# Moving the last zero fill behind the value gradient and w_q stores and giving six transfer engines more of it

## The chip, the cores and the metric

The kernel runs on one core of one Trainium2 chip. A core has five engines that take instructions (PE for matrix products, DVE and ACT for element-wise work, POOL, and SP), and sixteen transfer engines that carry out the DMAs which POOL, SP and ACT request. The metric is the device time of one execution in microseconds (us). The kernel before takes 594.82 us, the median of three runs (594.19 to 594.88).

## The reference

The reference is one decode step of a small transformer block, forward and backward, with batch and sequence of 1 and width D = 1024. Forward: six modulation vectors come from `silu(c) @ w_mod`; a layer norm scaled and shifted by two of them feeds attention of 32 query heads over 4 groups of cached keys and values, of which only the last 4096 of 65536 rows are used; the result goes through `wo`, a gate vector and a residual sum; a second layer norm feeds a gated feed-forward part (`sigmoid(h w_gate) * (h w_up)` times `w_down`) with its own gate and residual sum. Backward: given `grad_out`, it returns the output and the gradients by x, both caches, wq, wo, w_gate, w_up, w_down, c and w_mod.

Two things in this set the amount of data moved. The gradient of a weight matrix is, with one row of activations, an outer product of two vectors, and it has to be written in full. And the gradients of the two caches have the shape of the whole cache, (1, 4, 65536, 128) in bf16, 64 MB each, although only the last 4096 rows of each group are not zero. The other 61440 rows of each of 8 groups (15 MB a group, 120 MB in all) must be written as zeros. The kernel writes 186 MB in all and reads 79 MB.

## The kernel before, in words

**Zero fills.** The 120 MB of zeros are cut into pieces of 1 MB (`zleft`, filled at lines 149 to 156) and each is written by one DMA, or a few, that POOL requests. The helper `zero(n)` at line 185 takes n pieces from the list and issues them at the place in the program where it is called; tables such as `Z_N`, `Z_B`, `Z_FFN` and `Z_ROWS` (lines 51 to 59) say how many go at each place, so that the fills run beside loads and computation over the whole kernel. A fill has one of these forms: the plain one (line 209) writes 128 rows of 8 KB, cast from a tile of zeros in SBUF, eight rows to each of the sixteen transfer engines; the big one (line 203) copies 32 rows of 32 KB from a region of DRAM that was filled earlier (`zero_src`); six "narrow" ones (lines 191 to 199) use only 120 rows, shared out over fifteen engines, so that one engine is passed over. A fourth form, `uneven` (line 171), is in the file, and is used for the pieces whose running number stands in `UNEVEN`; that tuple is empty.

**How a piece is given to certain engines.** A DMA whose outermost count is not a multiple of sixteen is spread over fewer engines, beginning where the previous such DMA left off. Before an uneven or narrow fill POOL executes an instruction that puts this place back to the start (`reset_dge_cursor`, lines 174 and 192). `uneven` then issues very small DMAs only to move the place on (7 and 6 partitions), and larger ones that go to few engines.

**Order.** The whole kernel is written under a manual schedule: each engine executes its instructions in the order of the source, and waits are placed where data depend on each other. All transfers that POOL requests go through one software queue (q0), those of SP through a hardware queue (q1); both are served by the same sixteen transfer engines.

**The last quarter of the kernel**, in the order of POOL's requests: stores of outer products for w_down (`dwd`, line 1132), w_up and w_gate (`dw_rows`, line 1127), wo (`dwo`, line 1262) with fills between them (`Z_ROWS[0]` at line 1226, `Z_ROWS[1]` at line 1332); then the sections of w_mod (`sec`, line 1256) and the tiles of w_q (`dwq_tile`, line 1306); the value gradient (`grad_kv` at line 1431, stored by `kv_store`, line 1303, group 3 at line 1441); then the eighth section and the fourth w_q tile, `dwq_tile(3)` (line 1443); and last the key gradient (line 1481) with the other four w_q tiles and the first two w_mod columns (`s2`, line 1310) between its steps. From the third quarter of the key gradient on the stores are requested by SP (`tail = nc.sync`, line 1464). Buffers of the arena are used several times, so that an outer product can only be written by DVE when the store that last read its buffer has landed; the stores of the very end, after `dwq_tile(3)`, use buffers that nothing needs again.

At the end of the program the lines 1484 and 1485 issue whatever fills are left; in the kernel before none is left there.

Of the kernel before, what the change touches and what calls it, by code (L numbers as in the profile page):

```python
# [35 lines left out]
KIB = 512  # L36
SKIP = 4
NARROW = (15, 45, 75, 93, 103, 113)
UNEVEN = ()

def spread(total, n):
# [13 lines left out]
Z_FOLD = (1, 1, 2, 3)  # L56
Z_FFN = [(1, 0, 1)] + [(1, 1, 1)] * 4 + [(0, 2)]
Z_HAND = (1, 2, 1, 1, 1)
Z_ROWS = (1, 1, 0, 0, 0, 0, 0, 0)
JT = 3  # L60
JV = KD - JT
@with_exitstack
def kernel(
# [44 lines left out]
    def vt(shape, name, dt=FP32):  # L108
        return pool.tile(shape, dt, name=name)
# [4 lines left out]
    ZW = 4096  # L114
    zeros = vt([P, ZW // 2], "zeros", FP8)
# [30 lines left out]
    def as_rows(piece, n):  # L146
        return piece.rearrange("i (p x) -> (i p) x", p=n)
# [3 lines left out]
    zleft = []  # L151
# [11 lines left out]
    keep = [0]  # L163

    def dep(later, earlier):
        tc.add_manual_dep(later.ins, earlier.ins.name,
                          mybir.DependencyInfo(mybir.DependencyClass.Sync, mybir.DependencyReason.DATA),
                          reason="pace")

    def uneven(piece):
        parts, at = [], 0
        flat_f = piece.rearrange("i x -> (i x)").bitcast(FP32)
        nc.gpsimd.inc_swdge_sem([], [], mode="reset_dge_cursor")
        for n, x in ((7, 16), (34, 512), (6, 16), (68, 512)):
            parts.append(nc.gpsimd.dma_start(
                out=flat_f[at:at + 2 * n * x].rearrange("(t p x) -> p t x", t=2, p=n),
                in_=zeros[0:n, 0:x].rearrange("p (t x) -> p t x", t=1).broadcast_to([n, 2, x])))
            at += 2 * n * x
        left = P * ZW // 2 - at  # L180
        nc.gpsimd.dma_start(out=flat_f[at:].rearrange("(p x) -> p x", p=16),
                            in_=zero_src.rearrange("i x -> (i x)")[0:left // 2].bitcast(FP8).rearrange("(p x) -> p x", p=16))
        return parts[0]

    def zero(n, after=None, big=False):
        for _ in range(n):
            if len(zleft) <= keep[0]:
                return
            region, narrow_ = zleft.pop(0)
            first = None  # L190
            if narrow_:
                nc.gpsimd.inc_swdge_sem([], [], mode="reset_dge_cursor")
                n = nlen - ncount.pop()
                first = nc.gpsimd.dma_start(
                    out=rest[0:NS, 0:nlen * 128].rearrange("p (t x) -> p t x", t=2)[:, :, n * 64:(n + 1) * 64],
                    in_=zeros[0:NS, 0:64].rearrange("p (t x) -> p t x", t=1).broadcast_to([NS, 2, 64]))
                ins = nc.gpsimd.dma_start(
                    out=region[8:P, :].bitcast(FP32).rearrange("(t p) x -> p t x", t=2),
                    in_=zeros[0:60, :].rearrange("p (t x) -> p t x", t=1).broadcast_to([60, 2, ZW // 2]))
            elif 119 - len(zleft) in UNEVEN:  # L200
                first = ins = uneven(region)
            elif big and region.shape[0] == 1:
                ins = nc.gpsimd.dma_start(  # L203
                    out=as_rows(region, BIGP).bitcast(FP32),
                    in_=zero_src[:, 0:P * ZW // 4].rearrange("i (p x) -> (i p) x", p=BIGP).bitcast(FP8))
            else:
                if region.shape[0] == 1:
                    region = as_rows(region, P)
                ins = nc.gpsimd.dma_start(out=region.bitcast(FP32), in_=zeros[:, :])  # L209
            if after is not None:  # L210
                dep(first or ins, after)
# [26 lines left out]
    def mulv(out, a, b):  # L238
        return tt(out, a, b, ALU.mult)
# [46 lines left out]
    def outer_dve(out, col, b):  # L286
        return ts(out, b, col, ALU.mult)
# [52 lines left out]
    def bcast(col_bf, ncols, out_bf, engs):  # L340
        for k, j0 in enumerate(range(0, ncols, 4)):
            ps = new_ps("bc_ps")
            for jj in range(4):
                nc.tensor.matmul(ps[:, jj * P:(jj + 1) * P],
                                 lhsT=col_bf[:, j0 + jj:j0 + jj + 1].broadcast_to([P, P]), rhs=ident_bf[:, :],
                                 start=(jj == 0), stop=(jj == 3), skip_group_check=True)
            o = out_bf[:, j0 * P:(j0 + 4) * P]
            if engs[k % len(engs)] == "A":
                last = nc.scalar.copy(out=o, in_=ps[:, :])
            else:  # L350
                last = cp(o, ps[:, :])
        return last
# [774 lines left out]
    def dw_rows(k, j, off, outer):  # L1127
        t = ar(off, 7)
        outer(t, h2[:, j:j + 1], dug_row[k])
        nc.gpsimd.dma_start(out=(dwu_view, dwg_view)[k][:, j, :], in_=t)  # L1130
# [94 lines left out]
    dw_rows(0, 1, 16, outer_dve)  # L1225
    zero(Z_ROWS[0])
    bcast(dattn_bf, KD, dattn_b, "V")
# [28 lines left out]
    def sec(j):  # L1256
        w5 = g_t[j] if j < 6 else sec_t[j][:, 3 * D:4 * D]
        ttr(w5, w5, dmod_b4[:, 3 * D:4 * D], dcs[:, j:j + 1])
        outer_dve(sec_t[j], cs_col[:, j:j + 1], dmod_b4)
        nc.gpsimd.dma_start(out=dwm_view[:, j, 2 * D:6 * D], in_=sec_t[j])  # L1260

    def dwo(u):
        for a in range(4):
            outer_dve(wo_t[u][:, a, :], o_perm[:, 8 * a + u:8 * a + u + 1], dattn_b)
        nc.gpsimd.dma_start(out=wo_dram(out_5, u), in_=wo_t[u])
# [37 lines left out]
    def kv_store(og, home, g, queue=nc.gpsimd):  # L1303
        queue.dma_start(out=kv_out(og, g), in_=home[:, g, :])

    def dwq_tile(j, queue=nc.gpsimd):
        outer_dve(dwq_t[j], h1[:, j:j + 1], dq_b)
        queue.dma_start(out=dwq_view[:, j, :], in_=dwq_t[j])
# [7 lines left out]
    for b in range(2):  # L1316
        do4 = new_ps("do4")
        for i in range(KD):
            for a in range(4):
# [4 lines left out]
                       in_=do4.rearrange("q (a h r) -> q a h r", a=4, h=4))  # L1324
# [6 lines left out]
    dw_rows(0, 2, 40, outer_dve)  # L1331
    zero(Z_ROWS[1])
    dwo(2)
# [14 lines left out]
    dw_rows(0, 4, 32, outer_dve)  # L1348
    zero(Z_ROWS[2])
    dwo(3)  # L1350
    dw_rows(0, 5, 176, outer_dve)
    dw_rows(0, 6, 160, outer_dve)
    zero(Z_ROWS[3])
    dw_rows(0, 7, 40, outer_dve)
# [10 lines left out]
    dw_rows(1, 0, 64, outer_dve)  # L1365
    zero(Z_ROWS[4])
    dw_rows(1, 1, 72, outer_dve)
# [9 lines left out]
    dw_rows(1, 2, 80, outer_dve)  # L1377
    zero(Z_ROWS[5])
    dw_rows(1, 3, 88, outer_dve)
# [61 lines left out]
    kv_store(out_3, dv_home, 3)  # L1441
    sec(7)
    dwq_tile(3)
    x2 = vt([P, KD], "x2")
    mulv(x2, gb, ffn)
    addv(x2, x2, x1)
# [34 lines left out]
    grad_kv(dS, Q_bd, SCALE, dk_home, "AV", dk_between)  # L1481
    for g in range(G):
        kv_store(out_2, dk_home, g, nc.gpsimd if g < 1 else tail)
    keep[0] = 0
    zero(len(zleft))
    assert not zleft and not narrow and not jobs and not bq

# [28 lines left out]
```

## Time and profile before

| what | value |
|---|---|
| median of three runs | 594.82 us |
| the profiled execution's own time | 594.85 us |
| its span, first to last instruction | 593.0 us |
| PE, DVE, ACT, POOL busy | 72%, 60%, 42%, 25% |
| moved by the transfer engines | 246.58 MB, 416 GB/s in the mean |
| busy share of the transfer engines | 9 tenths or more in 38 of 40 slices |
| last instruction that computes | ends at 560.2 us |
| last store requested by POOL, by SP | 560.75 us, the three at the end from 560.27 us |

The span lies between the first and the last instruction; the execution's own time is 1.85 us more. The engines' busy shares are means over very different stages. In the line of the transfer engines a 9 is a slice of 14.8 us in which the sixteen were busy for 90% or more of the time; a share slightly above 1 comes from packets of one engine that overlap in the records. The last 30 us of the span hold no computation at all, only transfers.

### The profile page before, as it was taken

The page shows a single profiled execution, that of the slowest core. Times are in us where ns is not written, and L with a number is a line of the kernel's source. Part 1 is how long each engine was busy: PE and PEld are TensorE (multiplying, and loading weights), DVE is VectorE, ACT ScalarE, POOL GpSimd, SP SyncE. Part 2 cuts the span into 40 slices and gives each one's busy share as a digit, 9 for nine tenths or more (in the row PEclk, how much of TensorE's full clock was granted, in tenths as well). Part 3 has the DMA queues.
Part 4 walks back from the last instruction along what each step waited for, and adds up shares of the span by engine and source line. Part 5 has one row for each costly group of instructions (what it writes and reads, how often), then busy time and mean ns, then how long its engine had stood idle before and what let it go on. Part 6 is the DMA issues. An engine that isn't in the chain of part 4 may idle for free.

```text
span 593.0 us, 10218 instructions
## 1 busy us (share of the span) xinstructions
PE 425.7 (72%) x4196; PEld 244.2 (41%) x4196; DVE 354.7 (60%) x647; ACT 248.1 (42%) x398; POOL 145.9 (25%) x250
## 2 busy tenths in 40 slices
PE   3997679999999999997975756776665457555300
PEld 2784433322334545643443545555452345131000
DVE  3765679988830102039272866887986868678700
ACT  2479511554540103411133646665672455563200
POOL 3113213112122212122222412323222432332100
PEclk9998889999999999999997757777787657555555
DMA  8999999999999999999999999999999999999996
GB/s 347 421 420 421 423 465 426 424 426 424 425 405 456 425 438 421 408 418 439 423 395 411 420 410 408 397 409 409 423 421 428 424 424 423 418 422 415 417 416 289
DMA packets 32047, 246.58 MB, mean 416 GB/s; under 512 B 4781, under 2 KB 4781, under 8 KB 16688
## 3 DMA queue, kind: packets, MB, share of 16 engines
q0 software_dynamic: 26864, 225.46, 94.3%
q1 hardware_dynamic: 5088, 20.46, 9.6%
q8 instruction: 33, 0.54, 0.4%
q14 instruction: 14, 0.11, 0.1%
q10 hardware_dynamic: 48, 0.01, 0.0%
HBM read 79.17 MB, written 185.60 MB: 446 GB/s over the span
## 4 chain that ended last, share of the span: by engine, by line
DMA 40%; PE 23%; DVE 19%; issue 5%; ACT 5%; POOL 1%; ACTq 0%; DVEq 0%; POOLq 0%; SPq 0%
DMA out_dram<-out_dram 12%; DMA out_dram<-arena 11%; PE n_ps L737 9%; DVE arena L249 7%; DMA arena<-in_w_mod_dram 6%; DMA arena<-in_B_w_gate_dram 5%; DVE arena L253 4%; PE t_ps L685 4%; DVE scr L253 3%; DMA out_dram<-zeros 3%; DMA arena<-in_B_w_down_dram 3%; PE b_ps L796 2%; ACT arena L524 2%; DVE arena L236 2%; PE tp_k L503 1%
## 5 line engine op out<-in xcount | busy, mean ns | idle before, releaser
L796 PE MATMUL b_ps<-arena 128*128 128x512 bf16 x512 | 116.3, 379 | 1.1 <-ACT arena L940 1.1
L236 DVE TENSOR_TENSOR arena<-arena 128x2048 bf16<-128x2048 bf16 x64 | 77.7, 1224 | 9.0 <-PE n_ps L737 5.3
L940 ACT COPY arena<-tp_side 128x1024 bf16<-128x1024 bf16 x62 | 60.9, 1017 | 49.7 <-PE tp_side L939 48.9
L796 PEld LDWEIGHTS <-arena 128*128 128x128 bf16 x512 | 48.3, 98 | 56.6 <-issue 2.9
L737 PE MATMUL n_ps<-arena 128*128 128x512 bf16 x256 | 67.6, 388 | 3.6 <-DVE arena L236 3.3
L203 POOL DMA_DIRECT2D out_dram<-out_dram x72 | 35.6, 495 | 128.8 <-PE n_ps L737 52.4
L939 PE MATMUL tp_side<-ident_bf,arena 128*128 128x128 bf16 x496 | 50.6, 268 | 10.4 <-DVE arena L236 6.0
L939 PEld LDWEIGHTS <-arena 128*128 128x128 bf16 x496 | 41.7, 123 | 19.4 <-issue 8.9
L693 ACT CAST arena<-t_ps 128x512 bf16<-128x512 f32 x56 | 28.9, 598 | 39.9 <-PE t_ps L685 39.9
L253 DVE CUSTOM_DVE_ANT_0 arena<-arena,scr 128x1024 bf16<-128x1024 bf16 x35 | 40.8, 1220 | 0.2
L209 POOL DMA_DIRECT2D out_dram<-zeros x42 | 23.1, 554 | 55.0 <-DVE rows_all L236 25.1
L1295 PE MATMUL ps_kv<-arena 32*128 32x512 bf16 x64 | 25.2, 584 | 15.6 <-DVE arena L257 9.5
L253 DVE CUSTOM_DVE_ANT_0 scr<-arena,b1k 128x1024 bf16<-128x1024 bf16 x28 | 34.2, 1222 | 3.4 <-DMA arena<-in_B_w_down_dram 3.0
L1299 ACT ACTIVATE arena<-ps_kv 128x512 bf16<-128x512 f32 x48 | 25.0, 723 | 26.7 <-PE ps_kv L1295 17.1
L737 PEld LDWEIGHTS <-arena 128*128 128x128 bf16 x256 | 21.4, 99 | 35.8 <-issue 19.5
L249 DVE TENSOR_SCALAR arena<-arena,h 128x3584 bf16<-128x3584 bf16 (+1 forms) x24 | 28.3, 1192 | 12.0 <-DMA out_dram<-arena 12.0
L245 DVE CAST arena<-b_ps 128x512 bf16<-128x512 f32 x6 | 4.1, 692 | 48.8 <-PE b_ps L796 48.8
L685 PE MATMUL t_ps<-arena 128*32 128x512 bf16 x256 | 24.1, 399 | 2.8 <-ACT arena L760 2.8
L524 ACT COPY arena<-tp_wq 128x1024 bf16<-128x1024 bf16 x23 | 21.4, 1070 | 7.3 <-PE tp_wq L522 7.3
L1077 ACT COPY arena<-tp_ug 128x1024 bf16<-128x1024 bf16 x21 | 20.5, 1007 | 7.0 <-PE tp_ug L1076 7.0
L965 POOL DMA_DIRECT2D arena<-in_B_w_up_dram x14 | 10.7, 765 | 40.1 <-DVE dh2acc L253 26.7
L1295 PEld LDWEIGHTS <-arena 32*128 32x128 bf16 x64 | 6.8, 114 | 32.9 <-issue 32.0
(326 smaller groups left out, 664.4 us busy)
## 6 DMA issues: line engine op xcount, KB each, us to landing
out_dram<-zeros POOLq DMA_DIRECT2D x42, 1024.0 KB, 12.5
out_dram<-arena POOLq DMA_DIRECT2D x34, 1024.0 KB, 16.4
out_dram<-arena POOLq DMA_DIRECT2D x16, 896.0 KB, 17.1
arena<-in_A_wq_dram POOLq DMA_DIRECT2D x8, 1024.0 KB, 21.0
arena<-in_A_wo_dram POOLq DMA_DIRECT2D x8, 1024.0 KB, 13.8
arena<-in_w_mod_dram POOLq DMA_DIRECT2D x7, 1024.0 KB, 19.0
arena<-in_B_w_up_dram POOLq DMA_DIRECT2D x14, 512.0 KB, 9.9
arena<-in_B_w_gate_dram POOLq DMA_DIRECT2D x14, 512.0 KB, 14.6
```

The costliest lines, as they stand in the source:

```text
L203: ins = nc.gpsimd.dma_start(out=as_rows(region, BIGP).bitcast(FP32), in_=zero_src[:, 0:P * ZW // 4].rearrange("i (p x) -> (i p) x", p=BIGP ...
L236: return nc.vector.tensor_tensor(out=out, in0=a, in1=b, op=op)
L249: return nc.vector.tensor_scalar(out=out, in0=a, scalar1=s1, scalar2=None, op0=op0)
L253: return nc.vector.tensor_tensor_reduce(out=out, in0=w, in1=b, scale=1.0, scalar=0.0, op0=ALU.mult, op1=ALU.add, accum_out=acc)
L524: nc.scalar.copy(out=blk, in_=tp[:, :])
L685: nc.tensor.matmul(ps[32 * hh:32 * hh + 32, :].rearrange("p (j m) -> p j m", j=4), lhsT=N_sb[:, h * P + a:(h + 1) * P - 3 + a:4], rhs=a4[: ...
L693: nc.scalar.copy(out=o, in_=v)
L737: mm = nc.tensor.matmul(nbank[k][:, :], lhsT=k_nat[:, g, t_ * DH:(t_ + 1) * DH], rhs=vp[:, t_ % 2, 4 * k:4 * k + 4, :].rearrange("p h d -> ...
L796: mm = nc.tensor.matmul(bbank[p][k][:, :], lhsT=a4[:, p, h, :], rhs=wo_t[u][:, a, k * 512:(k + 1) * 512], start=(i == 0 and a == 0), stop= ...
L939: nc.tensor.transpose(tp[:, i * P:(i + 1) * P], blk[:, i * P:(i + 1) * P], ident_bf[:, :])
L940: nc.scalar.copy(out=blk if dst is None else dst, in_=tp[:, :])
L1295: nc.tensor.matmul(ps[:, :], lhsT=rows[r, t8 * P:(t8 + 1) * P], rhs=bd[r, :], start=True, stop=True, tile_position=(32 * tc_, 0))
```

## The change

The last of the 120 pieces is no longer written at line 1332, among the stores of the outer products for w_up and wo, in the plain form. It is written behind `dwq_tile(3)`, which follows the store of the fourth group of the value gradient, and in the uneven form. The uneven form itself is changed: it now consists of a reset instruction and five DMAs, of (7 partitions, 2 pieces each of 64 bytes), (2 partitions, 12 pieces each of 8 KB), (6 partitions, 2 pieces of 64 bytes), (4 partitions, 12 pieces of 8 KB), and a copy of the rest from DRAM in 16 rows of 28,568 bytes. So after 7 engines that get next to nothing 2 get 96 KB, after 6 more that get next to nothing 4 get 96 KB, and all sixteen get 28,568 bytes. In the plain form each of the sixteen gets 64 KB. The lines at the end that issued what was left go away. Nothing changes on PE, DVE, ACT or SP.

```diff
-UNEVEN = ()
+UNEVEN = (119,)
...
-Z_ROWS = (1, 1, 0, 0, 0, 0, 0, 0)
+Z_ROWS = (1, 0, 0, 0, 0, 0, 0, 0)
...
         nc.gpsimd.inc_swdge_sem([], [], mode="reset_dge_cursor")
-        for n, x in ((7, 16), (34, 512), (6, 16), (68, 512)):
+        for n, t, x in ((7, 2, 16), (2, 12, ZW // 2), (6, 2, 16), (4, 12, ZW // 2)):
             parts.append(nc.gpsimd.dma_start(
-                out=flat_f[at:at + 2 * n * x].rearrange("(t p x) -> p t x", t=2, p=n),
-                in_=zeros[0:n, 0:x].rearrange("p (t x) -> p t x", t=1).broadcast_to([n, 2, x])))
-            at += 2 * n * x
+                out=flat_f[at:at + t * n * x].rearrange("(t p x) -> p t x", t=t, p=n),
+                in_=zeros[0:n, 0:x].rearrange("p (t x) -> p t x", t=1).broadcast_to([n, t, x])))
+            at += t * n * x
         left = P * ZW // 2 - at
         nc.gpsimd.dma_start(out=flat_f[at:].rearrange("(p x) -> p x", p=16),
...
     sec(7)
     dwq_tile(3)
+    zero(len(zleft))
     x2 = vt([P, KD], "x2")
...
         kv_store(out_2, dk_home, g, nc.gpsimd if g < 1 else tail)
-    keep[0] = 0
-    zero(len(zleft))
     assert not zleft and not narrow and not jobs and not bq
```

## The prediction

> **What bounds the kernel now.** I read the page first (busy shares and the row of slices), then the order of POOL's and SP's requests near the two places of the change, then the windows of the last microseconds.
>
> ```profile
> PE 425.7 (72%) x4196; PEld 244.2 (41%) x4196; DVE 354.7 (60%) x647; ACT 248.1 (42%) x398; POOL 145.9 (25%) x250
> ...
> DMA  8999999999999999999999999999999999999996
> ...
> DMA packets 32047, 246.58 MB, mean 416 GB/s; under 512 B 4781, under 2 KB 4781, under 8 KB 16688
> ```
>
> No computing engine is near full; the transfer engines are, in every slice but the first and the last. All bytes are the same before and after, so the time can move only where transfer engines stand idle: in a hole, or at the end.
>
> ```profile
> 459.23 0.80 POOL L209 DMA_DIRECT2D out_dram<-zeros  x1
> ...
> 530.38 0.53 POOL L1304 DMA_DIRECT2D out_dram<-arena  x1 [1.66 <-DMA out_dram<-arena]
> 532.85 0.53 POOL L1304 DMA_DIRECT2D out_dram<-arena  x1 [1.94 <-DMA out_dram<-arena]
> ...
> 540.91 0.53 POOL L1308 DMA_DIRECT2D out_dram<-arena  x1 [2.10 <-DVE arena L249]
> 543.54 0.85 POOL L1308 DMA_DIRECT2D out_dram<-arena  x1 [2.10 <-DMA out_dram<-arena]
> ...
> 551.39 0.90 POOL L1308 DMA_DIRECT2D out_dram<-arena  x1 [1.92 <-DVE arena L249]
> 560.75 0.53 POOL L1304 DMA_DIRECT2D out_dram<-arena  x1 [8.46 <-DVE arena L249]
> ```
>
> The fill that moves is the request at 459.23; its new place is behind that at 540.91. POOL hands over one megabyte about every 2.5 us there (530.38 to 532.85), which is the pace of the transfers (1 MB at 420 GB/s is 2.50 us): it is held back by transfers that must finish first. With 16.4 us from issue to landing for a 1 MB store (the page's sixth part), some 16.4/2.5 = 6.6 transfers are in flight.
>
> ```profile
> 580.00:585.00 5.00, 0.00 (x0) 0.00 (x0) 0.00 (x0) 0.00 (x0) 0.00 (x0) 0.50 1.02 423
> ```
> ```profile
> 587.50:588.00 0.50, 0.00 (x0) 0.00 (x0) 0.00 (x0) 0.00 (x0) 0.00 (x0) 0.50 0.70 295
> 588.00:588.50 0.50, 0.00 (x0) 0.00 (x0) 0.00 (x0) 0.00 (x0) 0.00 (x0) 0.50 0.55 229
> 588.50:589.00 0.50, 0.00 (x0) 0.00 (x0) 0.00 (x0) 0.00 (x0) 0.00 (x0) 0.50 0.31 131
> 589.00:589.50 0.50, 0.00 (x0) 0.00 (x0) 0.00 (x0) 0.00 (x0) 0.00 (x0) 0.50 0.31 131
> 589.50:590.00 0.50, 0.00 (x0) 0.00 (x0) 0.00 (x0) 0.00 (x0) 0.00 (x0) 0.50 0.20 82
> 590.00:590.50 0.50, 0.00 (x0) 0.00 (x0) 0.00 (x0) 0.00 (x0) 0.00 (x0) 0.50 0.08 33
> 590.50:591.00 0.50, 0.00 (x0) 0.00 (x0) 0.00 (x0) 0.00 (x0) 0.00 (x0) 0.50 0.08 33
> ```
>
> The last two numbers of a window are the share of the sixteen engines and GB/s. The share times sixteen is how many still work: 11 at 587.75, 9 at 588.25, 5 at 588.75 and 589.25, 3 at 589.75, one or two to 590.92. So the engines do not finish together, and the last of them sets the time.
>
> The packet records of the trace say when each one ends. An engine takes eight pieces and one 4-byte completion from each transfer; from the end backwards, a packet belongs to the one that starts where it ends. The sixteen ends so found are 585.26, 585.41, 587.72, 587.87, 588.05, 588.06, 588.10, 588.38, 588.46, 588.86, 589.00, 589.10, 589.81, 589.94, 590.88 and 590.92; their mean is 588.49. Perfect balance would gain 2.43 us.
>
> Two marks tell something of which engines these are. The three row stores of 8 pieces (L294) use eight engines; linked on, these end at 587.72, 587.87, 588.05, 588.06, 589.00, 589.94, 590.88, 590.92: four early, four late. Of the other eight, two end at 585.3 to 585.4 and six between 588.10 and 589.81.
>
> **The change part by part.**
>
> *Bytes per engine.* An engine at full load moves 423/16 = 26.4 GB/s (window 580 to 585), so an 8 KB piece takes 0.310 us. The plain fill is 8 pieces on each engine. The uneven one is 28,568 bytes (3.49 pieces) on ten engines and 15.49 on six. Ten engines finish 4.51 x 0.310 = 1.40 us earlier, six 7.49 x 0.310 = 2.32 us later. The DRAM copy is priced like the rest: a 64 KB packet of such a fill takes 2.431 us in the records, eight pieces 2.48. The extremes are clear: no change can gain more than 1.40 us while any engine near 590.92 is among the ten, or lose more than 2.32.
>
> *Which six.* Counting partitions from the reset, the change passes over 7 engines, loads 2, passes over 6 and loads 4, so with numbers from 0 they are 7, 8, 15, 0, 1 and 2: four of the first eight and two of the other eight. The early ones at the end are also four and two. One more sign: in the narrow fill requested at 424.86 the five first engines after the reset get 256-byte pieces, and these packets start at 430.72, 431.08, 431.33, 432.54 and 432.64: three early, two more than a microsecond late. Three of the four loaded low engines (0, 1, 2) against two others (3, 4) fits that; the reverse would give two and three. I take it that the six are the early ones, and hold it for likely, not shown.
>
> *The sum.* The six early ones end at 585.26 to 588.06, so after at most 588.06 + 2.32 = 590.38. The latest of the ten ends at 590.92 - 1.40 = 589.52. The new end is 590.38, a gain of 0.54 us. Against the profiled execution's own 594.85 (span plus 1.85 us) that is 594.3; the median of the runs, 594.82, stands 0.03 lower, which changes nothing.
>
> *A rule that speaks against it.* The latest two ends, 590.88 and 590.92, belong to engines among the first eight, and the latest of the other eight is 589.81. The Trainium skill, page "DMA: Bandwidth & Descriptors", section "Latency and other measured facts", states that engines 7 and 15 are usually slower than the others, with an uncertain cause; both would be loaded here. By that rule 7 would be at 590.92 and the time 2.32 us longer; by the rows that I can read, no engine of the second eight is among the last three, so 15 at least does not stand out.
>
> *The earlier place.* The 1 MB taken out at 459.23 leaves 6.6 transfers, 16 us, of queued work; without one of them 14 us. That covers it, and the later requests move 2.5 us up until the fill comes back. I cost it at nothing. If that cover were gone, a hole of up to 2.5 us would open; nothing in the slices speaks for it.
>
> *POOL.* One request of 0.80 us becomes five, each between 0.53 and 1.24 us (rows from 540 to 552), and a reset: 2.7 to 6.2 us of POOL. Worse, each may have to wait for an older transfer as the rows above do, five times 2.5 us in place of once, which pushes the store of the fifth w_q tile from 543.54 to about 553 and those behind it as far. The last POOL store has 8.46 us of slack, and it waits for DVE until 560.2 anyway; nothing reads the buffers of these stores again, so DVE does not wait for POOL. What it costs is depth: five of some seven requests in flight hold together 1 MB, so queued work falls from 16 us to about 3 x 2.5 = 7 us for a while, and SP's stores come in from 548. Covered, and put at nothing; it ranges from nothing to the 2.5 us of one megabyte.
>
> **The rivals.**
>
> *A loaded engine is a late one (slower).* Place: the last 3 us. If any of the six ended after 590.92 - 2.32 = 588.60 before, the kernel is slower; seven engines did. To lose over 0.2% (1.19 us) it must have ended after 589.79; four did. With one of the last two the end is 593.24 and the time 597.2; with 589.94, 596.2. For it: the engines' numbers are not in the records, and the page named above. Against: four and two, three and two.
>
> *The six have more room than this execution shows (faster).* For a gain over 1.19 us the end must be at 589.73 or below, so the six must have ended by 587.41 before: the two at 585.3 do, four are 0.3 to 0.65 us too late. The three runs differ by 0.69 us, so ends may shift by that much. The limit is the ten, 1.40 us: 593.4.
>
> *The pieces do not go to six engines.* If all sixteen share them, or the place does not go back to the start, nothing moves: 594.8. Against it: the narrow fills' 256-byte packets come in five groups, as their count of five partitions says.
>
> *A hole in the queue.* The depth falls too far at POOL's five requests, and up to 2.5 us are lost: 597.3. Against it: 25 us of stores are still to come after the last request at 560.75.
>
> **How the numbers follow.** The six early ones loaded, 594.3: 0.38. No special load, 594.8: 0.04. More room, 593.4: 0.22. A late engine loaded, 596.2 to 597.2 (this is also where the page's rule would end): 0.30. A hole, 597.3: 0.06. About 0.2% (1.19 us) is what a measurement of this kernel can tell from no change. Faster by more than that is 0.22, within it 0.38 + 0.04 = 0.42, slower 0.30 + 0.06 = 0.36. The range runs from 593.2, which is the limit of the ten (593.4) with 0.2 us of the runs' own difference, to 597.2, with a late engine; the likeliest case's own range is 593.7 to 595.0, its four latest engines shifting by 0.65 us either way.
>
> **What would show it.** In the last windows the share stays near 1 longer and falls more steeply: from 589.5 on about four engines instead of one to three, and nothing after 590.4. Packet records: ten engines end at 586.7 to 589.5, six at 587.6 to 590.4. If two or fewer engines work on alone after 591, a late one was loaded. Near 545 to 555 the share must stay at 1.0; a lower one is the hole. POOL's five requests stand between 541 and 553. The prediction is wrong if the ends are not the same from execution to execution, or if the loaded six are others than I took.

## The result and the profile after

The changed kernel takes 603.98 us (median of six runs, 601.29 to 606.93) against 594.85 us for the kernel before: a ratio of 1.0154, with a 95% interval from 1.0125 to 1.0182. The forecast was 594.3 us in a range of 593.2 to 597.2, with slower at 0.36. The kernel is 9.1 us slower, beyond the range. The profiled execution took 604.16 us, with a span of 602.1.

The profile page of the changed kernel: engines, the row of the transfer engines in 40 slices, and the packets.

```profile
span 602.1 us, 10223 instructions
...
PE 426.4 (71%) x4196; PEld 241.6 (40%) x4196; DVE 354.8 (59%) x647; ACT 248.0 (41%) x398; POOL 150.5 (25%) x254
...
DMA  8999999999999999999999999999999999999991
...
DMA packets 32447, 246.58 MB, mean 409 GB/s; under 512 B 5221, under 2 KB 5221, under 8 KB 17128
```

PE, DVE and ACT do the same work as before, and the bytes are the same. There are 400 packets more, and 440 more under 512 bytes. The last slice, 15 us long, is busy for one tenth, where before it was six tenths.

Windows over the end of the changed kernel; the last two numbers are the share of the sixteen transfer engines and GB/s.

```profile
580.00:585.00 5.00, 0.00 (x0) 0.00 (x0) 0.00 (x0) 0.00 (x0) 0.00 (x0) 0.50 1.02 429
585.00:587.50 2.50, 0.00 (x0) 0.00 (x0) 0.00 (x0) 0.00 (x0) 0.00 (x0) 0.50 0.95 403
587.50:590.00 2.50, 0.00 (x0) 0.00 (x0) 0.00 (x0) 0.00 (x0) 0.00 (x0) 0.50 0.54 226
590.00:592.00 2.00, 0.00 (x0) 0.00 (x0) 0.00 (x0) 0.00 (x0) 0.00 (x0) 0.50 0.28 119
592.00:594.00 2.00, 0.00 (x0) 0.00 (x0) 0.00 (x0) 0.00 (x0) 0.00 (x0) 0.50 0.07 29
594.00:596.00 2.00, 0.00 (x0) 0.00 (x0) 0.00 (x0) 0.00 (x0) 0.00 (x0) 0.50 0.06 25
596.00:598.00 2.00, 0.00 (x0) 0.00 (x0) 0.00 (x0) 0.00 (x0) 0.00 (x0) 0.50 0.05 20
```

One engine of sixteen is 0.0625: from 592.24 on a single engine works, until 597.68 by the packet records. The mean of the sixteen ends is 589.76, against 588.49 before. So the last packet ends 6.8 us later than before (590.92): the transfer engines as a group lost 1.27 us, and 5.5 us are one engine that is far behind the others.

The other 2.3 us of the longer span come after the last packet. Before, the span ended 2.1 us after it; now it ends 4.5 us after it. The instruction records show why. A DRAIN, the instruction of POOL that stands behind its last request at the end of the program, ends at 601.36, which is 3.7 us after the last packet of POOL's queue (597.68), and the span ends 0.8 us after that. Before, POOL's queue had its last packet at 584.14 and the DRAIN ended at 587.71, while SP's queue worked until 590.92; so POOL's end was hidden behind SP's transfers.

Windows from 555 to 570, first before and then in the changed kernel, where the fill is carried out: the engines are busy in both, yet the rate falls from 412 to 417 GB/s to 389 to 408.

```profile
555.00:560.00 5.00, 1.86 (x5) 0.40 (x3) 5.00 (x8) 1.56 (x3) 0.00 (x0) 0.50 1.01 415
560.00:565.00 5.00, 0.00 (x0) 0.00 (x0) 0.21 (x1) 0.00 (x0) 0.53 (x1) 0.50 1.01 417
565.00:570.00 5.00, 0.00 (x0) 0.00 (x0) 0.00 (x0) 0.00 (x0) 0.00 (x0) 0.50 1.01 412
```

```profile
555.00:560.00 5.00, 1.03 (x3) 0.12 (x1) 4.37 (x7) 0.98 (x2) 0.59 (x1) 0.50 1.03 406
560.00:565.00 5.00, 0.00 (x0) 0.00 (x0) 0.00 (x0) 0.00 (x0) 0.54 (x1) 0.50 1.04 389
565.00:570.00 5.00, 0.00 (x0) 0.00 (x0) 0.00 (x0) 0.00 (x0) 1.06 (x2) 0.50 1.05 408
```

POOL's requests in the changed kernel, in order: start, duration, line, and in brackets the idle time before and what ended it.

```profile
542.34 0.60 POOL L176 DMA_DIRECT2D out_dram<-zeros  x1 [1.80 <-DMA out_dram<-arena]
544.95 1.61 POOL L176 DMA_DIRECT2D out_dram<-zeros  x1 [2.01 <-DMA out_dram<-arena]
547.48 0.54 POOL L176 DMA_DIRECT2D out_dram<-zeros  x1 [0.92 <-DMA out_dram<-arena]
550.15 1.33 POOL L176 DMA_DIRECT2D out_dram<-zeros  x1 [2.13 <-DMA out_dram<-arena]
553.01 0.54 POOL L181 DMA_DIRECT2D out_dram<-out_dram  x1 [1.53 <-DMA out_dram<-arena]
557.32 0.59 POOL L1308 DMA_DIRECT2D out_dram<-arena  x1 [3.77 <-DVE arena L249]
561.49 0.54 POOL L1312 DMA_DIRECT2D out_dram<-arena  x1 [3.58 <-DMA out_dram<-arena]
566.21 0.53 POOL L1312 DMA_DIRECT2D out_dram<-arena  x1 [4.19 <-DMA out_dram<-arena]
...
570.24 0.53 POOL L1304 DMA_DIRECT2D out_dram<-arena  x1 [2.77 <-DMA out_dram<-zeros]
```

Each of the five requests of the fill has to wait, whatever its size, as the prediction feared. The store that was requested at 543.54 before comes at 557.32, and the last one at 570.24 where it was 560.75; that one waits for a request of the fill itself.

```profile
526.51 18.15 DMA out_dram<-arena
544.95 24.72 DMA out_dram<-zeros
```

These are the last two lines of the chain of waits: the second request, 192 KB, takes 24.72 us from 544.95 until it has landed.

The packet records show where an engine fell behind. They name no engine: the rows below are linked by their times, with gaps of up to 117 ns between them, and that they belong to the engine that ends last is likely, not shown. Start in us, queue (0 is POOL's, 1 is SP's), bytes, duration in ns; an 8-KB packet takes 311 ns in the median before from 540 on, and none from 555 to 575 took over 430.

```
559.127  0  8192   519
559.656  1  4096   473
560.161  0  8192  1722
562.000  0  8192   727
562.738  1  8192   720
563.486  1  8192   691
564.206  1  8192  1004
565.229  1  8192   807
```

Such packets follow one another for some 7 us, those of SP's stores among them. By their durations they are not pieces of the fill, which take 322 or 348 ns: from 552 to 580 POOL's queue has 73 such 8-KB records here, where the fill has 72 pieces, 131 in e1 below, whose plain fill has 128, and 6 in e9, whose fill has none of 8 KB. So packets of ordinary stores were held up. The engine that ends last begins its own twelve pieces of the fill only at 569.88, and they run without a gap to 575.98. It reaches its share of the copy at 576.59, when the fifteen others had theirs between 564.85 and 571.93.

### The profile page after: what moved, and what is told of

It reads as the page before. It is cut to its first block, busy times and chain, and to the rows that moved or that the text cites. A ratio compares the mean times of both kernels' runs of the same rounds, so it can differ in the third digit from the quotient of the medians.

```text
span 602.1 us, 10223 instructions
## 1 busy us (share of the span) xinstructions
PE 426.4 (71%) x4196; PEld 241.6 (40%) x4196; DVE 354.8 (59%) x647; ACT 248.0 (41%) x398; POOL 150.5 (25%) x254
## 4 chain that ended last, share of the span: by engine, by line
PE 38%; DMA 26%; DVE 18%; ACT 6%; issue 5%; POOL 1%; ACTq 0%; POOLq 0%; DVEq 0%
PE b_ps L796 15%; DMA out_dram<-arena 10%; PE n_ps L737 9%; DMA out_dram<-zeros 6%; DMA arena<-in_B_w_gate_dram 5%; DMA arena<-in_w_mod_dram 4%; DVE arena L253 4%; DVE arena L236 4%; PE t_ps L685 3%; DVE arena L249 2%; DVE scr L253 2%; ACT arena L524 2%; PE tp_k L503 1%; PE w_ps L466 1%; PE ok L633 1%
## 5 line engine op out<-in xcount | busy, mean ns | idle before, releaser
L796 PE MATMUL b_ps<-arena 128*128 128x512 bf16 x512 | 118.6, 384 | 1.1 <-ACT arena L940 1.1
L796 PEld LDWEIGHTS <-arena 128*128 128x128 bf16 x512 | 49.0, 99 | 58.0 <-issue 5.4
L939 PE MATMUL tp_side<-ident_bf,arena 128*128 128x128 bf16 x496 | 48.1, 260 | 11.7 <-DVE arena L236 5.8
L939 PEld LDWEIGHTS <-arena 128*128 128x128 bf16 x496 | 39.7, 119 | 20.6 <-issue 11.2
L737 PEld LDWEIGHTS <-arena 128*128 128x128 bf16 x256 | 21.4, 99 | 35.7 <-issue 19.4
L249 DVE TENSOR_SCALAR arena<-arena,cs_col 128x4096 bf16<-128x4096 bf16 (+1 forms) x16 | 16.0, 1020 | 8.5 <-DMA out_dram<-arena 8.4
```

Source lines behind the costliest of these rows:

```text
L249: return nc.vector.tensor_scalar(out=out, in0=a, scalar1=s1, scalar2=None, op0=op0)
L737: mm = nc.tensor.matmul(nbank[k][:, :], lhsT=k_nat[:, g, t_ * DH:(t_ + 1) * DH], rhs=vp[:, t_ % 2, 4 * k:4 * k + 4, :].rearrange("p h d -> ...
L796: mm = nc.tensor.matmul(bbank[p][k][:, :], lhsT=a4[:, p, h, :], rhs=wo_t[u][:, a, k * 512:(k + 1) * 512], start=(i == 0 and a == 0), stop= ...
L939: nc.tensor.transpose(tp[:, i * P:(i + 1) * P], blk[:, i * P:(i + 1) * P], ident_bf[:, :])
```

## The experiments

Intervals of single ratios reach 0.1 to 0.4% to either side, for most kernels 0.6 to 1.2 us; differences below that say nothing.

**Place and form apart.** e1 leaves the place and takes the plain form; e2 leaves the form and takes the old place.

```diff
 # e1                                # e2
-UNEVEN = (119,)                     -Z_ROWS = (1, 0, 0, 0, 0, 0, 0, 0)
+UNEVEN = ()                         +Z_ROWS = (1, 1, 0, 0, 0, 0, 0, 0)
                                     -    zero(len(zleft))
```

> The last fill stands at its new place, behind the fourth w_q tile, but in the plain form: one request, 64 KB to each engine. Theory L (one of the six loaded engines is a late one, and its twelve pieces set the end): 594.8, within 0.7 us of the kernel before. Theory D (five requests in place of one make the queue shallow and open a hole): 594.8 too, since there is one request. Theory P (the late place alone costs): 600 or more.

> The uneven form with its five requests stands at the old place, line 1332, among the stores of the outer products. Theory L: the load falls on the same engines, so about what the changed kernel takes, 601 to 605. Theory D: the queue holds 16 us of work there and nothing near its end, so 594 to 597. Theory P: 594 to 595.

e1: 594.59 us, ratio 1.000 (0.9989 to 1.0012). e2: 597.91 us, 1.0055 (1.004 to 1.007). The place alone costs nothing, the form alone 3.1 to 3.2 us, and both together 9.1: what the form costs depends on what runs beside it. In e2 the latest engines end at 593.73 and 593.36, 2.8 and 2.5 us after the latest of before (590.92 and 590.88), near the 2.32 us of the load.

**The load.** e3 keeps five requests and the copy at the new place, but gives all sixteen the same. e4 leaves out one engine: two requests of 7 engines pass over one more, so 7, 8, 0, 1 and 2 are loaded by the count.

```diff
-        for n, t, x in ((7, 2, 16), (2, 12, ZW // 2), (6, 2, 16), (4, 12, ZW // 2)):
+        for n, t, x in ((7, 2, 16), (16, 2, 1536), (6, 2, 16), (16, 3, ZW // 2)):     # e3
+        for n, t, x in ((7, 2, 16), (2, 12, ZW // 2), (7, 2, 16), (3, 12, ZW // 2)):  # e4
```

> The new place, five requests of the same sizes (0.9, 192, 0.8, 384 and 446 KB), but the two large ones are spread over all sixteen engines, 12 KB and 24 KB each, so that no engine is loaded more than another. Theory L: 594.5 to 596. Theory D: 601 to 605, as the changed kernel. Theory P: 600 or more.

> As the changed kernel, but the third request passes over seven engines and the fourth loads three, so that by the counting from 0 engines 7, 8, 0, 1 and 2 are loaded and 15 is not; all sixteen get 34,704 bytes in the copy. If the late engine is number 15: 595 to 597, and no engine works on alone for more than 2 us. If it is 0, 1, 2, 7 or 8: 602 to 605. Theory D: 602 to 605.

e3: 596.17 us, 1.0034 (1.0022 to 1.0047). e4: 602.56 us, 1.0118 (1.0091 to 1.0144), and one engine alone at the end again (599.46, the next 594.94). So number 15 is not what made the kernel slow. By the Trainium skill, page "DMA: Bandwidth & Descriptors", section "Latency and other measured facts", engines 7 and 15 are usually slower; 602.56 without loading 15 does not bear that out for 15, and no run here tells of 7 alone.

**What the loaded pieces read.** e5 takes the pieces of the loaded engines from partitions 36 apart in place of 0, 1, 2, 3. e6 copies the 96-KB shares of the loaded engines from DRAM, as one row each, without any 8-KB piece from SBUF. e7 takes the load away: its pieces are cut to 64 bytes, and the copy writes the rest. e8 is a single request of 16 rows of 8 pieces, all read from partitions 0 to 15, without copy, small requests and load.

```diff
# e5
-                in_=zeros[0:n, 0:x].rearrange("p (t x) -> p t x", t=1).broadcast_to([n, t, x])))
+                in_=(zeros[0:36 * n - 35:36, 0:x] if n < 6 else zeros[0:n, 0:x]).rearrange("p (t x) -> p t x", t=1).broadcast_to([n, t, x])))
# e6
-        for n, t, x in ((7, 2, 16), (2, 12, ZW // 2), (6, 2, 16), (4, 12, ZW // 2)):
+        for n, t, x in ((7, 2, 16), (2, 1, 12 * ZW // 2), (6, 2, 16), (4, 1, 12 * ZW // 2)):
...
+                src = zero_src.rearrange("i x -> (i x)")[0:n * x // 2].bitcast(FP8).rearrange("(p x) -> p x", p=n)
# e7
-        for n, t, x in ((7, 2, 16), (2, 12, ZW // 2), (6, 2, 16), (4, 12, ZW // 2)):
+        for n, t, x in ((7, 2, 16), (2, 12, 16), (6, 2, 16), (4, 12, 16)):
# e8
-        for n, t, x in ((7, 2, 16), (2, 12, ZW // 2), (6, 2, 16), (4, 12, ZW // 2)):
+        for n, t, x in ((16, 8, ZW // 2),):
...
-        nc.gpsimd.dma_start(out=flat_f[at:].rearrange("(p x) -> p x", p=16),
```

> As the changed kernel, but the twelve pieces are read from partitions 36 apart (0 and 36; 0, 36, 72 and 108) in place of 0 and 1, and 0 to 3. Theory H (the loaded engines all read a few neighbouring partitions of SBUF, and an engine whose way leads there is held up): the packets of 470 to 1722 ns between 559 and 570 go, 597 to 598.5, as the uneven form at its old place. Theory Y (each piece for few engines leaves a 4-byte packet on every other one, some 350 of them, and these hold an engine up): 601 to 605 and the long packets stay.

> As the changed kernel, but the 96 KB of a loaded engine are one row read from DRAM in place of twelve pieces read from SBUF: neither the reads of few partitions nor the 312 4-byte packets of the two large requests. The load stays. Theories H and Y: 597 to 598.5. If the long packets and over 601 stay, both fall, and it is the load at the late place itself (theory S: beside SP's stores).

> The requests of the changed kernel with the twelve pieces cut to 64 bytes; the rest of the megabyte (65,144 bytes for each of sixteen engines) is the copy from DRAM. The 350 4-byte packets stay, load and reads of few partitions go. Theory Y: the long packets stay; without the load 596 to 600. Theories H and S: 594.5 to 595.5.

> The new place, one request of 16 rows by 8 pieces, read from partitions 0 to 15 alone: the same 64 KB for each engine, no 4-byte packets, reads of few partitions by all. Theory H: long packets and lower GB/s near 560, 596 to 600. Theories Y and S: 594.5 to 595.5, as the plain form at this place.

e5: 599.34 us, 1.0089 (1.0063 to 1.0115). e6: 596.34 us, 1.0022 (1.0009 to 1.0036). e7: 599.88 us, 1.0083 (1.0066 to 1.01). e8: 596.78 us, 1.004 (1.0025 to 1.0054). Reading from neighbouring partitions costs 4.6 us (604.0 against e5), and 2.2 us where there is nothing else (e8 against e1). And something in the small requests costs, for e7 has no load and no such reads. What the load alone costs these runs do not settle. e5 has it and e7 has not, and e5's median is 0.5 us lower; but of the two profiled executions that of e5 is 2.0 us longer (602.21 against 600.18), with the last packet at 595.73 against 593.68. e5 also lies between its two expectations, 597 to 598.5 and 601 to 605.

e6 did not do what it was meant to. Its two requests for the 96-KB rows appear as sixteen packets of 12,288 bytes and sixteen of 24,576, and all sixteen engines get the same. So e6 loads no engine, and its expectation that the load stays does not hold. A small outermost count alone does not keep a request on few engines.

The packet lines of e7 and of e6 show what the small requests can cost: a request to few engines leaves a 4-byte packet for each of its pieces on every engine that it passes over.

```profile
DMA packets 32447, 246.58 MB, mean 412 GB/s; under 512 B 5293, under 2 KB 5293, under 8 KB 17200
```
```profile
DMA packets 32095, 246.58 MB, mean 415 GB/s; under 512 B 4909, under 2 KB 4909, under 8 KB 16816
```

For e7 that is 14 engines by 12 pieces, 12 by 12, 9 by 2 and 10 by 2, together 350. In e6 only the 9 by 2 and 10 by 2 are left, 38: had its rows gone to two and four engines, there would be 14 + 12 more. Windows of e7 beside that:

```profile
555.00:560.00 5.00, 1.08 (x3) 0.15 (x1) 4.41 (x7) 1.03 (x2) 0.59 (x1) 0.50 1.01 406
560.00:565.00 5.00, 0.00 (x0) 0.00 (x0) 0.00 (x0) 0.00 (x0) 0.54 (x1) 0.50 1.03 402
565.00:570.00 5.00, 0.00 (x0) 0.00 (x0) 0.00 (x0) 0.00 (x0) 1.59 (x3) 0.50 1.07 394
570.00:575.00 5.00, 0.00 (x0) 0.00 (x0) 0.00 (x0) 0.00 (x0) 0.00 (x0) 0.50 0.98 378
```

The share is full and the rate is down. The 4-byte packets themselves last 9 ns each: 350 of them are 3.2 us, 0.2 us on each engine. So their own duration is not the price.

**The form taken apart.** e9 makes the four small requests even (16 partitions, one 64-byte piece each: no 4-byte packets beyond the usual). e10 is e6 with the passing-over changed, so that the rows were to go to other engines (3, 4, 5, 6, 9 and 10 by the count). e11 is e6 at the old place, e12 is e7 at the old place.

```diff
+        for n, t, x in ((16, 1, 16), (16, 1, 16), (16, 1, 16), (16, 1, 16)):                  # e9
-        for n, t, x in ((7, 2, 16), (2, 1, 12 * ZW // 2), (6, 2, 16), (4, 1, 12 * ZW // 2)):  # e6
+        for n, t, x in ((3, 2, 16), (4, 1, 12 * ZW // 2), (2, 2, 16), (2, 1, 12 * ZW // 2)):  # e10
-Z_ROWS = (1, 0, 0, 0, 0, 0, 0, 0)                                                            # e6, e7
+Z_ROWS = (1, 1, 0, 0, 0, 0, 0, 0)                                                            # e11, e12
-    zero(len(zleft))
```

> The four requests ahead of the copy become four of 16 partitions with one 64-byte piece each; the copy from DRAM writes the rest (16 rows of 65,472 bytes). So five requests at the new place, the copy, no uneven load and none of the 350 four-byte packets that requests on fewer than sixteen engines leave on the others. e7, with those packets, took 599.9. If the packets are what cost in e7: 594.5 to 595.5. If it is POOL's five requests one behind another (each holding a place in its queue) or the copy: 599 to 600. Half and half: 597.

> e6 (loads of 96 KB as one row each, read from DRAM) with the passing-over changed from 7 and 6 to 3 and 2 engines, so that by the count the loaded ones are 3, 4, 5, 6, 9 and 10, none of those of e6 (7, 8, 15, 0, 1, 2). e6 took 596.3. If e6's six hold late engines and these hold fewer: 593.5 to 595. If any six loaded engines hold late ones: 596 to 597.5. If e6's 1.6 us came from its requests and not from the load: 596.3 again.

> e6 at the old place, behind the outer products for w_up. e2, the changed form as it is at the old place, took 597.9. If the load on late engines makes all of e2's 3.2 us: 597.5 to 598. If its reads of 8-KB pieces from few partitions and the four-byte packets make about half of it, as e6 against the changed kernel suggests: 596 to 597. If the load costs nothing at the old place: 594.6.

> e7 (12 pieces cut to 64 bytes, the rest by the copy from DRAM: no load, all 350 four-byte packets) at the old place. e7 at the new place took 599.9. If the packets cost wherever they are: 599 to 600. If they cost because POOL's queue is held up at the new place, where SP's stores run ahead meanwhile: 594.5 to 595.5.

e9: 596.31 us, 1.0022 (1.0011 to 1.0032). e10: 596.54 us, 1.0027 (1.0013 to 1.004). e11: 596.94 us, 1.0042 (1.0023 to 1.0062). e12: 596.34 us, 1.0027 (1.0013 to 1.004). e10 and e11 copy their rows as e6 does, in sixteen equal packets each, so none of e6, e9 and e10 loads an engine, and all three take the same time. No run loads six other engines. The 350 packets cost 3.6 us at the new place (e7 against e9) but nothing at the old one: e12 has them and takes 596.34, while e11, an even fill there with 38 of them, takes 596.94. e12 thus lies between its two expectations.

**Which part of the rest.** e13 has the copy alone, one request for the whole megabyte; e14 is e7 with 6 pieces in place of 12.

```diff
+        for n, t, x in ():                                                  # e13
-        for n, t, x in ((7, 2, 16), (2, 12, 16), (6, 2, 16), (4, 12, 16)):  # e7
+        for n, t, x in ((7, 2, 16), (2, 6, 16), (6, 2, 16), (4, 6, 16)):    # e14
```

> The four small requests are left away; the whole megabyte is the one copy from DRAM in 16 rows of 64 KB, at the new place. e9, the same with four 64-byte requests ahead of it, took 596.3; the plain fill at this place (e1) took 594.6. If the five places in POOL's queue are what cost in e9: 594.3 to 595.2. If the copy does (long packets ahead of the last stores): 596 to 596.6.

> e7 with 6 pieces in place of 12 in the second and fourth request: 14 x 6 + 12 x 6 + 38 = 194 four-byte packets in place of 350, everything else as in e7 (599.9; e9 with none: 596.3). If each packet costs alike: 596.3 + 3.6 x 194/350 = 598.3. If the cost comes with requests that go to few engines, whatever their pieces: 599.5 to 600. If it sets in only with many: 596 to 597.

e13: 596.11 us, 1.0024 (1.001 to 1.0037). e14: 598.14 us, 1.006 (1.0038 to 1.0081). The first 1.5 us come with the copy, and four more requests add 0.2. The copy's own packets have the price that the prediction gave them, 2431 ns for 64 KB; but while they run, 21 packets of 8 KB from 555 to 565 take over 430 ns, where e1 has none. With 194 packets in place of 350 the added cost is 1.8 us in place of 3.6, as if it went with their number; but the four runs of e14 reach from 596.80 to 599.64, and up to 1.5 us of e7's 3.6 may be the early hole told of at the end.

**Which queue ends last.** The table has, from the records of each profiled execution, the last packet of POOL's and of SP's queue, the end of POOL's DRAIN, and the span, all in us.

| kernel | extra 4-byte packets of the last fill | POOL's queue | SP's queue | DRAIN | span |
|---|---|---|---|---|---|
| before | none | 584.14 | 590.92 | 587.71 | 593.04 |
| e9, new place | none | 586.82 | 591.00 | 590.52 | 593.10 |
| e14, new place | 194 | 590.30 | 591.22 | 594.01 | 594.79 |
| e7, new place | 350 | 593.68 | 591.23 | 597.37 | 598.14 |
| e12, old place | 350 | 585.45 | 592.26 | 589.16 | 594.36 |
| the changed kernel | 350 | 597.68 | 597.68 | 601.36 | 602.15 |

In every one of the profiled executions the DRAIN ends 3.55 to 3.73 us after the last packet of POOL's queue. The span ends 2.1 us after the last packet of SP's queue or 0.8 us after the DRAIN, whichever is later. At the new place the 4-byte packets set POOL's queue back: SP's queue had moved 3.29 MB of its 8.39 by 570 in e9, 3.88 in e14 and 4.17 in e7, so it runs ahead of POOL's. POOL's queue then ends near SP's or after it, and its longer way to the end, 4.5 us in place of 2.1, is what counts. At the old place POOL's queue ends 6.8 us before SP's, and the packets cost nothing. So 2.3 us of the 9.1 are a tail that SP's requests do not have.

**Near, or sharing a way.** e15 and e16 are e5 with other distances between the partitions read: 0, 4, 8, 12, and 0, 32, 64, 96.

```diff
# e15
-                in_=(zeros[0:36 * n - 35:36, 0:x] if n < 6 else zeros[0:n, 0:x]).rearrange("p (t x) -> p t x", t=1).broadcast_to([n, t, x])))
+                in_=(zeros[0:4 * n - 3:4, 0:x] if n < 6 else zeros[0:n, 0:x]).rearrange("p (t x) -> p t x", t=1).broadcast_to([n, t, x])))
# e16
+                in_=(zeros[0:32 * n - 31:32, 0:x] if n < 6 else zeros[0:n, 0:x]).rearrange("p (t x) -> p t x", t=1).broadcast_to([n, t, x])))
```

> e5 with the loaded pieces read from partitions 4 apart (0, 4, 8, 12) in place of 36 apart; the changed kernel, with 0, 1, 2, 3, took 604.0, e5 599.3. If what costs is that the sources lie near each other: 602 to 604. If it is that four neighbouring partitions share something that 0, 4, 8 and 12 do not share: 598.5 to 600. The Trainium skill, page SBUF — State Buffer, section Door 1: The DMA port swizzle, says that partitions 0 to 3 are reached through one port and 4 to 7, 8 to 11 and 12 to 15 each through another; by that rule this run goes with e5.

> e5 with the loaded pieces read from partitions 32 apart (0, 32, 64, 96) in place of 36 apart. If what costs is nearness: 598.5 to 600, as e5 (599.3). If sources share something at a distance of 32 and not of 36, the two loaded engines meet on one and the four on two: between e5 and the changed kernel (604.0), 600.5 to 602.5. The Trainium skill, page SBUF — State Buffer, section Door 1: The DMA port swizzle, says that a step of 32 partitions stays on the same port and a step of 64 does not; by that rule this run lies between.

e15: 599.14 us, 1.0072 (1.0055 to 1.0089). e16: 604.08 us, 1.0138 (1.0099 to 1.0178). The ends of the two, e15 first:

```profile
590.00:592.00 2.00, 0.00 (x0) 0.00 (x0) 0.00 (x0) 0.00 (x0) 0.00 (x0) 0.50 0.19 78
592.00:594.00 2.00, 0.00 (x0) 0.00 (x0) 0.00 (x0) 0.00 (x0) 0.00 (x0) 0.50 0.03 8
594.00:596.00 2.00, 0.00 (x0) 0.00 (x0) 0.00 (x0) 0.00 (x0) 0.00 (x0) 0.50 0.00 0
```
```profile
590.00:592.00 2.00, 0.00 (x0) 0.00 (x0) 0.00 (x0) 0.00 (x0) 0.00 (x0) 0.50 0.47 197
592.00:594.00 2.00, 0.00 (x0) 0.00 (x0) 0.00 (x0) 0.00 (x0) 0.00 (x0) 0.50 0.24 102
594.00:596.00 2.00, 0.00 (x0) 0.00 (x0) 0.00 (x0) 0.00 (x0) 0.00 (x0) 0.50 0.09 37
596.00:598.00 2.00, 0.00 (x0) 0.00 (x0) 0.00 (x0) 0.00 (x0) 0.00 (x0) 0.50 0.04 16
```

Nearness is out: 4 apart is as good as 36 apart, and 32 apart is as bad as next to each other. Reading from certain partitions together is what costs. That is the rule of the Trainium skill, page "SBUF — State Buffer", section "Door 1: The DMA port swizzle (why `[64,N]` ≈ `[32,N]`)": four neighbouring partitions, and those 32 further on, are reached through one port, and a step of 4 leads to another. The four times 604.0, 599.3, 599.1 and 604.1 agree with it in kind. In size e16 was to lie between. It did not by its median; but its profiled run holds the early hole told of at the end, and one of its four runs took 600.27. The expectation also counted each request by itself: the two loading requests were under way together (requested at 545.14 and 550.34, the first landed at 570.52), and then up to four engines read from partitions 0 and 32.

The landings of the copy in the trace, one for each engine, say the same without the medians. The last engine's comes 4.7 us after the one before it in the changed kernel, 4.2 in e4 and 2.7 in e16, where four to six engines can read through one port at once, and 0.1 in e5 and 0.3 in e15, where at most two do. So the single engine far behind comes with the shared sources.

**The sum of the parts.** Each row is one edit away from the one above it, at the new place.

| kernel | us | step |
|---|---|---|
| plain fill (e1) | 594.59 | |
| one copy from DRAM (e13) | 596.11 | +1.5 |
| four small even requests ahead of it (e9) | 596.31 | +0.2 |
| the requests to few engines, 350 4-byte packets (e7) | 599.88 | +3.6 |
| 12 pieces of 8 KB for six engines, sources apart (e5) | 599.34 | -0.5 |
| sources next to each other (the changed kernel) | 603.98 | +4.6 |

The +3.6 holds the 2.3 us of POOL's tail and perhaps up to 1.5 us of the early hole. The -0.5 is the load together with a smaller copy, and by the profiled executions it is +2.0; the others stand as they are.

## Why the prediction was wrong

*What bounds the kernel now* held in part. No computing engine changed and all bytes are the same; but of the 9.1 us only 6.8 lie before the last packet. The other 2.3 come after it, where no transfer is at work.

*The earlier place* held: costed at nothing, e1 measures 594.59.

*Bytes per engine* is the first step that failed. It priced each loaded piece at 0.310 us and the copy "like the rest", and held for clear that no change can lose more than 2.32 us. The bytes an engine gets did not decide. The copy cost 1.5 us, with other packets longer beside it. And the loaded pieces, with their sources on partitions 0 to 3, cost 4.6 us, through packets of ordinary stores on one engine. In the rows shown above packets of 472 to 1722 ns took the place of 8-KB packets of some 309 and one 4-KB packet of 159; about 4.5 us of those 7 is excess. Together with the 2.32 us of load on an engine that would else have ended near 590.9, this makes 597.7, where the last engine ends. That addition is argued: no record says which engine it is.

*Which six* was "likely, not shown", and it stays so: no run loads six other engines. The rival that a late engine is loaded was at hand, and e2 ends as that rival says, with two engines 2.5 and 2.8 us after those of before; but e12, at the same place and without load, ends 1.3 us later too (592.26), so not all of that is load. Its price, 2.32 us at most, is not what the 9.1 us hang on. The sign named for it, two or fewer engines alone after 591, did come after 592.24; but a held-up engine gives the same sign.

*The sum*, a gain of 0.54 us, could not be seen anywhere: adding the load to e7 gives -0.5 us by the medians, within the runs' uncertainty, and +2.0 by the profiled executions. The sum also took the way from the last packet to the end as fixed, and it went from 2.1 to 4.5 us.

*POOL*, "covered, and put at nothing", is the second step that failed. The waits came as described, five times, and the stores behind were pushed from 543.54 to 557.32. Even so the five requests alone cost 0.2 us (e9 against e13), so this price was right. What the step did not see is what small uneven requests leave in the queue: 350 packets of 4 bytes, up to 3.6 us. They put POOL's queue, which had ended 6.8 us before SP's, last, and then its DRAIN sets the end. Why an engine that works through 4-byte packets lets SP's run ahead is argued, from the turns that it takes between the two queues; no run took SP's stores away.

*A hole in the queue* was to cost up to 2.5 us. None opened in the changed kernel near its new place: the share stays at 1.01 to 1.05 from 545 to 570.

## What to carry to other kernels

A transfer's cost is not its bytes on each engine: when the transfer engines bound, count its packets, also the empty ones on engines that it leaves out, and look which partitions its sources lie on, since several engines that read through one way slow the transfers beside them. Look also at which queue ends last: here the program ended 4.5 us after POOL's last packet and 2.1 us after SP's. To load engines unevenly, read each one's share from partitions that do not share a port (4 apart was as good as 36 apart here); even so nothing was won by it in any of these kernels. And check in the packet records that the engines were loaded as meant, as e6 was not. A spread in the ends of engines in one execution does not mean that moving that work will bring them together.

## What the runs showed of the hardware

- A request for few engines leaves one 4-byte packet for each of its pieces on each of the other engines. Counted in the changed kernel: 350 more than the completions explain.
- A request of two or four 96-KB rows from DRAM to DRAM is not given to two or four engines: e6 and e10 have sixteen packets of 12,288 and sixteen of 24,576 bytes.
- One engine takes packets of POOL's queue and of SP's by turns. While six engines read from partitions 0 to 3, single packets of ordinary stores took up to 1722 ns in POOL's queue and 473 to 1004 ns in SP's.
- POOL's DRAIN at the end of the program ends 3.55 to 3.73 us after the last packet of POOL's queue, in all profiled executions. It lengthens the program only where that queue ends last or nearly so.
- A request of POOL can be held for 7.9 us (the first of the two in the row of e7 below). In the profiled runs of e4, e5, e7 and e16 this opened a hole near 470, far ahead of the changed place, and some 0.35 MB less were moved by 480 than in the changed kernel (0.8 us; 1.4 us by 540). The profiled run of e11, whose fill stands there, has a hold of 4.7 us and a larger hole. Requests of POOL in e7, then in e1, and the windows from 465 to 475 of e7 and of e1, where the third pair of numbers is DVE's and the fifth POOL's:

```profile
464.95 8.38 POOL L1265 DMA_DIRECT2D out_dram<-arena  x2 [0.17 <-DVE dq_bf L245]
```
```profile
464.78 0.60 POOL L1265 DMA_DIRECT2D out_dram<-arena  x1 [0.17 <-issue]
```
```profile
465.00:470.00 5.00, 1.00 (x9) 0.66 (x7) 5.00 (x11) 1.86 (x3) 5.00 (x1) 0.50 1.01 426
470.00:475.00 5.00, 0.00 (x0) 0.00 (x0) 4.00 (x8) 0.00 (x0) 5.00 (x5) 0.50 0.87 365
```
```profile
465.00:470.00 5.00, 2.76 (x25) 2.35 (x23) 5.00 (x10) 3.43 (x4) 2.49 (x4) 0.72 1.02 427
470.00:475.00 5.00, 0.00 (x0) 0.00 (x0) 4.28 (x8) 0.00 (x0) 2.59 (x4) 0.62 1.00 421
```

DVE is busy without a gap from 465 to 470 in e7 (5.00 us of 5). The Trainium skill, page "SBUF — State Buffer", section "A bandwidth-pool intuition that's wrong (but worth ruling out)", says that a transfer requested by GpSimd beside a DVE copy waits for descriptors that GpSimd cannot write until DVE lets go of a shared port. The row agrees with that, but e1 has nearly the same DVE work (5.00 us there too) and no such hold, so when it strikes is open. It is not in the profile of the kernel before, nor in that of the changed kernel. Only profiled runs show it, so the medians of e4, e5, e7, e11 and e16 may hold some of it: 1.5 us in e7 against e9 by 540.
